# Eight one-bank PSUM tiles instead of four two-bank ones, a third score buffer and an even spread of q·k products in a fused attention and MLP kernel

## The chip, the cores and the metric

One core of a Trainium2 chip runs the whole program. The metric is the device time of one execution in microseconds (us). The engines are TensorE (PE, with its weight loads as PEld), VectorE (DVE), ScalarE (ACT), GpSimd (POOL) and SyncE (SP), which here only issues transfers. TensorE's clock has two levels, 1.2 and 2.4 GHz; the profile gives the granted share (1.00 is 2.4 GHz).

## The reference

Batch 4, 12 heads, 448 tokens, head size 64; then a feed-forward layer of 1792 tokens, 768 to 2048 to 768. All in fp32.

```
scores = scale * q @ k^T                                  # per batch and head
scores = einsum('bhij,hg->bgij', scores, w_pre)           # heads mixed
attn   = softmax(scores, axis=-1)                         # + 1e-9 in the denominator
attn   = einsum('bhij,hg->bgij', attn, w_post)            # heads mixed again
x      = (attn @ v) laid out as (1792, 768)
h      = relu(x @ w_in);  out = (s * h * h + b) @ w_out
```

## The kernel before

**Attention** is a software pipeline. The tokens of a batch are cut into 4 chunks of up to 120 queries (16 chunks), a chunk into blocks of 10 queries (180 blocks), and a step takes two blocks (90 steps). For a chunk, `qk` multiplies q and k of two heads into the PSUM tile `sc`, and `s_copy` (L479, ACT) scales them into the SBUF tile `S`, which holds a chunk's 12 heads in two buffers. `relayout` (L523) moves a block from `S` by DMA into one of six tiles `blk`, so that heads and queries lie on partitions; even blocks go through SP's queue, odd ones through POOL's, three steps ahead of use. A step s then does, in the order in which the code is written:

- `premix` (L533, PE): `blk` times the Kronecker matrix of w_pre into the PSUM tile `pm` (two blocks of columns, b = 0 and 1)
- `av` (L496, PE): the product with v for an earlier chunk, into the PSUM tile `xp`, which takes the slot of the *next* step's `pm`; `tr_q`, `tr_k` (L440, L420, PE): transposes of q and k into slot D
- `maxima` (L542, DVE, one reduction for b = 0 and one for b = 1), `exponential` b = 0 (L548, ACT), `weights` of the step before (L559 reciprocal on DVE, L561 on POOL)
- `x_copies` (L506 on ACT, then L507 on DVE adds the other half), copies of the transposes (L452 ACT, L455 DVE), `exponential` b = 1
- `postmix` (L575, PE) of step s - 2 into `po` (slot C), `evacuate` (L586, DVE, twice), `qk` into slot D, whose copy comes at the start of the next step; `totals` (L554, POOL), DMA issues, and at most two operations of a weight conversion (DVE).

Each engine takes its instructions in this order. The table `plan` says which q·k product, transpose, load and product with v belongs to which step.

**PSUM** has eight banks. The kernel has four slots A to D, each *one tile* `[P, 2, 512]` of two banks. Waits are made per tile: who writes one half of a tile waits for the reader of the other half if that comes earlier in the program.

**The MLP** follows, in two rounds r of 8 blocks f of 128 hidden units. fp32 weights are split into two fp32r parts by a chain of eight DVE operations a unit (`conversion`, L155 to L179), 64 units in 16 buffers. `gemm1_part` (L261) makes `ph` (18 matmuls), `relu2` reads it (L269 ACT and three more ACT operations), `gemm2` (L315) makes `po` for a block of 128 tokens (24 matmuls), read by ACT (L322, r = 0) or DVE (L326, r = 1). `bank` hands out the two halves of a slot in turn.

Of the kernel before, what the change touches and what calls it, by code (L numbers as in the profile page):

```python
# [2 lines left out]

# [18 lines left out]
def talking_heads_attention__then__act_relu2_kernel(  # L22
# [54 lines left out]
    NU_EARLY, NU_TAIL = 7, 6  # L77
# [11 lines left out]
    sp = att.enter_context(tc.tile_pool(name="sp", bufs=2))  # L89
# [150 lines left out]
    turn = {"slot": 0, "half": 1, "ops": 0}  # L240

    def slot(tag, name):
        return ps.tile([P, 2, 512], F32, tag=tag, name=name, bufs=1)
# [44 lines left out]
    def head_piece():  # L288
# [3 lines left out]
        if kc == 0:  # L292
            if f % 2 == 0:
                head_t["two"] = slot("DA"[f // 2], f"ph_head{f}")
            head_t[f] = head_t["two"][:, f % 2]
# [8 lines left out]
    def gemm2(r, oh, its):  # L304

        if len(its) > 1:
            turn["half"] = 1
# [106 lines left out]
    def tr_k(b, p, tr):  # L414
        nat = nat_t.pop((b, p))
        for c in range(NC):
            for r in range(2):
                if c < KC[r]:
                    for e in range(2):
                        nc.tensor.matmul(  # L420
                            tr[64 * e:64 * e + 64, r, 64 * c:64 * c + 64],
# [5 lines left out]
        return [(t[:, HK * r:HK * r + 64 * KC[r]], tr[:, r, :64 * KC[r]]) for r in range(2)]  # L427

    def tr_q(ci, p0, p1, tr):
# [7 lines left out]
        for p in range(p0, p1):  # L437
            for r in range(2):
                for e in range(2):
                    nc.tensor.matmul(  # L440
                        tr[64 * e:64 * e + 64, r, (p - p0) * m[r]:(p - p0 + 1) * m[r]],
# [5 lines left out]
             tr[:, r, :(p1 - p0) * m[r]].rearrange("q (a n) -> q a n", n=m[r]))  # L447
# [11 lines left out]
    def qk(ci, p, sc):  # L459
# [5 lines left out]
        for c0, c1 in ((0, 64), (64, n)):  # L465
            for e in range(2):
                nc.tensor.matmul(  # L467
                    sc[c0:c1, e, :S], qt[64 * e:64 * e + 64, p, c0:c1], kt[64 * e:64 * e + 64, :],
                    start=True, stop=True,
                )  # L470

    def s_copy(ci, p, sc, apart=False):
        n = chunks[ci][2]
        s = s_t[ci]
        if apart:
            nc.scalar.activation(s[:n, 2 * p, :], sc[:n, 0, :S], AF.Copy, scale=SCALE)
            nc.vector.tensor_scalar_mul(s[:n, 2 * p + 1, :], sc[:n, 1, :S], SCALE)
        else:
            nc.scalar.activation(s[:n, 2 * p:2 * p + 2, :], sc[:n, :, :S], AF.Copy, scale=SCALE)  # L479

    def av(ci, p, xp):
# [4 lines left out]
        for i, c in enumerate((0, 3, 1, 2)):  # L486
            for r in range(2):
                for e in range(2):
                    k0, h = 64 * r, 2 * p + e
                    o = xp[64 * e:64 * e + 64, r, :2 * m]  # L490
# [9 lines left out]
    def x_copies(ci, p, xp):  # L500
# [4 lines left out]
        x = [xp[:, r, :BI * nb].rearrange("q (b t i) -> q b t i", b=2, i=UI) for r in range(2)]  # L505
# [383 lines left out]
```

## Time and profile before

| | |
|---|---|
| time, three runs | 1013.74 us (median), 1009.86, 1019.23 |
| profiled execution | 1011.67 us, of which span 1009.9 us |
| PE busy | 835.9 us (83% of the span) |
| DVE, ACT, POOL busy | 537.6 (53%), 436.7 (43%), 243.9 (24%) |
| chain that ended last | PE 60%, DVE 13%, ACT 11%, issue 7%, DMA 7% |
| first `pm`, start of the last step's `pm` | 22.99 us, 446.63 us |
| first matmul of the MLP without the attention beside it | 476.57 us |

Shares of busy time are averages over the two halves. Idle time that a row names is that of one engine just before an instruction, with what ended it. A step of the attention is read as the distance from one `pm` to the next.

### The profile page before, as it was taken

What the parts mean: (1) busy time and instruction counts of PE and PEld (TensorE: products, weight loads), DVE (VectorE), ACT (ScalarE), POOL (GpSimd) and SP (SyncE); (2) the same over time, 40 slices, a digit from 0 to 9 for tenths busy, and PEclk for the clock granted to TensorE, in tenths of its full rate; (3) what the DMA queues carried; (4) which work ended last, traced back from release to release, by engine and by line L of the source; (5) the groups of instructions that cost most, each with busy time, mean ns of one, the idle gap of its engine ahead of it and who ended that gap; (6) DMA issues with size and microseconds to landing.
All of it is one profiled execution on the core that took longest, in us unless ns stands there. A gap on an engine that the chain in (4) does not pass through costs nothing.

```text
span 1009.9 us, 31606 instructions
## 1 busy us (share of the span) xinstructions
PE 835.9 (83%) x13544; PEld 682.5 (68%) x13544; DVE 537.6 (53%) x1186; ACT 436.7 (43%) x935; POOL 243.9 (24%) x446
## 2 busy tenths in 40 slices
PE   7777787677876787795998899799999898996998
PEld 3344555444554554474887789788888787896887
DVE  4465666456656666676930579354039209936111
ACT  4554564455555564544566660110156667300000
POOL 2333343234433433431223230000013223200000
PEclk9899999999999999998999999899999999998999
DMA  5675456644666456741330223425104201434221
GB/s 126 175 183 153 116 130 168 164 143 120 160 167 172 121 146 152 210 121 50 102 104 14 87 79 86 133 91 176 41 15 148 87 1 50 151 107 137 82 93 41
DMA packets 108830, 116.12 MB, mean 115 GB/s; under 512 B 48526, under 2 KB 101130, under 8 KB 108690
## 3 DMA queue, kind: packets, MB, share of 16 engines
q1 hardware_dynamic: 92460, 83.86, 30.4%
q0 software_dynamic: 7120, 18.67, 7.1%
q10 hardware_dynamic: 9110, 11.59, 3.2%
q8 instruction: 106, 1.74, 0.7%
q14 instruction: 34, 0.28, 0.1%
HBM read 58.99 MB, written 16.52 MB: 75 GB/s over the span
## 4 chain that ended last, share of the span: by engine, by line
PE 60%; DVE 13%; ACT 11%; issue 7%; DMA 7%; SPq 2%; ACTq 0%; DVEq 0%
PE ph L261 22%; PE po L315 22%; DVE st L542 5%; PE pm L533 5%; PE sc L467 4%; DMA blk<-S 3%; PE xp L496 3%; ACT e L548 3%; ACT xs L506 2%; ACT h L269 2%; DVE xs L507 2%; DVE A L586 1%; DMA part<-ob 1%; ACT S L479 1%; PE po L575 1%
## 5 line engine op out<-in xcount | busy, mean ns | idle before, releaser
L315 PE MATMUL po<-w,g 128*128 128x384 f32 x1344 | 242.8, 341 | 25.4 <-DVE acc L326 13.3
L315 PEld LDWEIGHTS po<-w,g 128*128 128x128 f32 x1344 | 236.2, 191 | 31.9 <-DVE acc L326 16.5
L261 PE MATMUL ph<-x,w 128*128 128x448 f32 x810 | 170.6, 367 | 20.8 <-ACT h L269 20.8
L261 PEld LDWEIGHTS ph<-x,w 128*128 128x128 f32 x810 | 151.5, 189 | 38.7 <-ACT h L269 28.6
L548 ACT ACTIVATE e<-pm,st 128x448 f32<-128x448 f32 x180 | 113.9, 633 | 115.9 <-DVE st L559 108.6
L279 POOL TENSOR_TENSOR g<-h,g 128x448 fp32r<-128x448 f32 x64 | 79.6, 1243 | 343.7 <-ACT g L278 321.9
L467 PE MATMUL sc<-Tk,Tq 64*64 64x448 f32 (+2 forms) x768 | 96.8, 565 | 54.7 <-ACT Tk L452 22.0
L542 DVE TENSOR_REDUCE st<-pm 128x1 f32<-128x448 f32 x180 | 103.8, 618 | 42.8 <-PE pm L533 32.1
L533 PE MATMUL pm<-blk,wpre 64*64 64x448 f32 x720 | 92.3, 565 | 27.2 <-DVE xs L507 22.1
L496 PEld LDWEIGHTS xp<-A,v 64*64 64x64 f32 x3072 | 77.9, 136 | 45.5 <-issue 33.7
L561 POOL TENSOR_SCALAR W<-kron,st 128x60 f32<-128x60 f32 x180 | 76.4, 431 | 122.7 <-DVE st L559 121.7
L575 PE MATMUL po<-W,e 60*64 60x60 f32 x5040 | 95.4, 219 | 8.8 <-issue 6.9
L586 DVE COPY A<-po 128x420 f32<-128x420 f32 x180 | 98.3, 589 | 7.8 <-PE po L575 7.6
L575 PEld LDWEIGHTS po<-W,e 60*64 60x64 f32 x5040 | 89.5, 136 | 18.4 <-issue 17.1
L479 ACT ACTIVATE S<-sc 110x896 f32<-110x896 f32 (+1 forms) x86 | 79.5, 924 | 44.0 <-DMA blk<-S 22.0
L507 DVE TENSOR_TENSOR xs<-xp,xs 128x110 f32<-128x110 f32 (+1 forms) x96 | 34.0, 354 | 116.3 <-ACT xs L506 116.3
L496 PE MATMUL xp<-A,v 64*64 64x110 f32 (+3 forms) x3072 | 85.8, 250 | 3.8 <-ACT e L548 2.6
L261 PE MATMUL ph<-xg,w 128*128 128x448 f32 x288 | 64.8, 382 | 17.7 <-DVE xg L237 10.0
L237 DVE TENSOR_TENSOR x<-xraw,x 128x448 fp32r<-128x448 f32 x36 | 22.1, 638 | 101.4 <-ACT x L228 101.4
L533 PEld LDWEIGHTS pm<-blk,wpre 64*64 64x64 f32 x720 | 24.1, 135 | 76.6 <-DVE xs L507 49.6
L261 PEld LDWEIGHTS ph<-xg,w 128*128 128x128 f32 x288 | 56.3, 198 | 25.0 <-ACT h L269 10.3
L269 ACT ACTIVATE h<-ph 128x448 f32<-128x448 f32 x61 | 33.1, 542 | 85.3 <-PE ph L261 85.2
(69 smaller groups left out, 787.1 us busy)
## 6 DMA issues: line engine op xcount, KB each, us to landing
blk<-S SPq DMA_DIRECT2D x89, 210.0 KB
blk<-S POOLq DMA_DIRECT2D x83, 210.0 KB, 4.7
raw<-in_moe_w_in_dram SPq DMA_DIRECT2D x32, 384.0 KB
raw<-in_moe_w_out_dram SPq DMA_DIRECT2D x32, 384.0 KB
xraw<-xd SPq DMA_DIRECT2D x48, 224.0 KB
part<-ob ACTq DMA_DIRECT2D x28, 192.0 KB
acc<-part SPq DMA_DIRECT2D x28, 192.0 KB
out_dram<-acc ACTq DMA_DIRECT2D x28, 192.0 KB
```

Source lines behind the costliest of these rows:

```text
L261: nc.tensor.matmul(ph[:, :S], w[:, i, c0:c0 + P], x[:, y, :], start=(kc == 0 and m == 0), stop=(kc == NKC - 1 and m == 2),)
L279: nc.gpsimd.tensor_tensor(out=g[:, 1, c0:c0 + S], in0=h, in1=g[:, 0, c0:c0 + S].bitcast(F32), op=ALU.subtract)
L315: nc.tensor.matmul(po[:, :NO], g[:, x, c0:c0 + P], w[:, y, :], start=(f == 0 and m == 0), stop=(f == NF - 1 and m == 2),)
L467: nc.tensor.matmul(sc[c0:c1, e, :S], qt[64 * e:64 * e + 64, p, c0:c1], kt[64 * e:64 * e + 64, :], start=True, stop=True,)
L479: nc.scalar.activation(s[:n, 2 * p:2 * p + 2, :], sc[:n, :, :S], AF.Copy, scale=SCALE)
L496: nc.tensor.matmul(o, vt[k0:k0 + 64, e, c, :], x, start=(i == 0), stop=(i == NC - 1),)
L533: nc.tensor.matmul(pm[64 * c:64 * c + 64, b, :S], wpre[k, :], blk[k, :], start=True, stop=True)
L542: nc.vector.tensor_reduce(out=st[:, b:b + 1], in_=pm_t[s][:, b, :S], axis=AX.X, op=ALU.max, negate=True)
L548: nc.scalar.activation(e[:, b, :], pm_t[s][:, b, :S], AF.Exp, bias=st[:, b:b + 1], accum_out=st[:, 2 + b:3 + b])
L561: nc.gpsimd.tensor_scalar(w[:, b, :], kron2, st[:, 6 + b:7 + b], None, op0=ALU.mult)
L575: nc.tensor.matmul(po[64 * c:64 * c + 64, r, m * U:m * U + U], e[64 * r:64 * r + U, b, j0:j0 + 64], w[64 * r:64 * r + U, b, :], start=True ...
L586: nc.vector.tensor_copy(a_t[ci].rearrange("q m h j -> q (m h) j")[:, :, UI * r:UI * r + UI], po_t[t // 2][:, t % 2, :n].rearrange("q (m i) ...
```

## The change

- A slot is now a list of two tiles of one bank each; `bank` hands out eight single banks in turn. `maxima` becomes `maximum(s, b)`, and the second stands behind the reciprocal on DVE.
- `x_copies` returns its two parts with keys 0 and 2, copies of transposes get key 1, `s_copy` key 3; what a step has of them is done in the order of the keys. `s_copy` is now two ACT operations of 448 columns in place of one of 896.
- `S` has three buffers (21.5 KB a partition more); 2 instead of 6 weight units (`NU_TAIL`) lie in the space of q and k, the others in the space of the attention.
- The q·k products of chunks 2 to 15 are spread evenly from step 2 to step 80, with their transposes and loads. Before, each chunk had a step without a product and mostly one with two (`more`).

By the two plans, after the change 39 of the 90 steps have one product and nothing else beside their work, 13 have one k transpose, 11 a q transpose; 10 have two things at once (two products, two `av`, two transposes). The first 8 steps have no `av`, steps 81 to 83 no product, and the last 6 carry the first matmuls of the MLP.

```
-    sp = att.enter_context(tc.tile_pool(name="sp", bufs=2))
+    sp = att.enter_context(tc.tile_pool(name="sp", bufs=3))
...
-    NU_EARLY, NU_TAIL = 7, 6
+    NU_EARLY, NU_TAIL = 7, 2
...
+    def one(tag, name):
+        return ps.tile([P, 512], F32, tag=tag, name=name, bufs=1)
     def slot(tag, name):
-        return ps.tile([P, 2, 512], F32, tag=tag, name=name, bufs=1)
+        return [one(f"{tag}{i}", f"{name}_{i}") for i in range(2)]
...
     def bank(name):
-        turn["half"] ^= 1
-        if turn["half"] == 0:
-            turn["two"] = next_slot(name)
-        return turn["two"][:, turn["half"]]
+        turn["bank"] += 1
+        return one(banks[(turn["bank"] - 1) % len(banks)], name)
...
-            nc.scalar.activation(s[:n, 2 * p:2 * p + 2, :], sc[:n, :, :S], AF.Copy, scale=SCALE)
+            for e in range(2):
+                nc.scalar.activation(s[:n, 2 * p + e, :], sc[e][:n, :S], AF.Copy, scale=SCALE)
...
-        nc.scalar.activation(o, x[0], AF.Copy)
-        nc.vector.tensor_tensor(out=o, in0=x[1], in1=o, op=ALU.add)
-        stores.append((xd[b][p, :, n0:n0 + n], xs[:, :n]))
+        def add():
+            nc.vector.tensor_tensor(out=o, in0=x[1], in1=o, op=ALU.add)
+            stores.append((xd[b][p, :, n0:n0 + n], xs[:, :n]))
+        return (0, lambda: nc.scalar.activation(o, x[0], AF.Copy)), (2, add)
...
-        where = [lo + x for x in ([0, 1, 2, 2, 3, 4] if hi - lo < 5 else range(6))]
...
+            step = 2 + ((ci - 2) * NP + p) * (LAST_QK - 2) // ((NCH - 2) * NP - 1)
+            if (step, "qk") in plan:
+                plan[step, "more"] = plan.pop((step, "qk"))
+            at(step, "qk", ci, p)
...
         if s < NS:
-            maxima(s)
+            open_softmax(s)
+            maximum(s, 0)
             exponential(s, 0)
         if 0 <= s - 1 < NS:
             weights(s - 1)
-        for tag in list(users):
-            for f in users.pop(tag):
-                f()
+        if s < NS:
+            maximum(s, 1)
+        for _, f in sorted(sum(users.values(), []), key=lambda x: x[0]):
+            f()
         if s < NS:
             exponential(s, 1)
```

The order of DVE around step 80, a step with one product and one `av`: first the kernel before, then the changed one (`st` maxima and sums, `pm` scores in PSUM, `xp` and `xs` the product with v, `A` the mixed attention; `waits` names whose semaphore is waited for).

```order
L542 TENSOR_REDUCE st_80_7472<-pm_80_7450 128x1 [waits DVE_49,PE_49]
L542 TENSOR_REDUCE st_80_7472<-pm_80_7450 128x1
L559 RECIPROCAL st_79_7396<-st_79_7396 128x2 [waits Pool_49]
L507 TENSOR_TENSOR xs_12_5_7481<-xp_12_5_7455,xs_12_5_7481 128x2x11x5 [waits DMAHW0_49,Activation_49]
L586 COPY A_13_7121<-po_78_7485 128x84x5 [waits PE_49]
L586 COPY A_14_7515<-po_78_7485 128x84x5
```

```order
L546 TENSOR_REDUCE st_80_7933<-pm_80_0_7908 128x1 [waits DVE_49,PE_49]
L563 RECIPROCAL st_79_7852<-st_79_7852 128x2 [waits Pool_49]
L546 TENSOR_REDUCE st_80_7933<-pm_80_1_7909 128x1 [waits PE_49]
L508 TENSOR_TENSOR xs_12_5_7932<-xp_12_5_1_7915,xs_12_5_7932 128x2x11x5 [waits DMAHW0_49,PE_49,Activation_49]
L590 COPY A_13_7557<-po_78_0_7945 128x84x5 [waits PE_49]
L590 COPY A_14_7976<-po_78_1_7946 128x84x5 [waits PE_49]
```

The reciprocal has moved between the two maxima, and each of these now has a PSUM tile and a wait of its own.

The order of ACT in a step with a k transpose (`Tk` is the transposed k, `tr` its PSUM tile), before and changed:

```order
L548 ACTIVATE e_62_5943,st_62_5942<-pm_62_5904,st_62_5942 128x448 [waits PE_49,DVE_49,Activation_49,Pool_49]
L506 ACTIVATE xs_9_4_5951<-xp_9_4_5909 128x2x11x5 [waits DMAHW0_49,PE_49]
L452 ACTIVATE Tk_3_5_5941<-tr_62_5926 128x192 [waits DVE_49]
L548 ACTIVATE e_62_5943,st_62_5942<-pm_62_5904,st_62_5942 128x448
L479 ACTIVATE S_12_5687<-sc_12_4_5988 110x896 [waits PE_49]
```

```order
L552 ACTIVATE e_61_6226,st_61_6225<-pm_61_0_6183,st_61_6225 128x448 [waits DVE_49,Activation_49,Pool_49]
L511 ACTIVATE xs_9_3_6207<-xp_9_3_0_6189 128x2x11x5 [waits DMAHW6_49,PE_49]
L451 ACTIVATE Tk_3_5_6224<-tr_61_1_6209 128x192 [waits PE_49]
L552 ACTIVATE e_61_6226,st_61_6225<-pm_61_1_6184,st_61_6225 128x448 [waits DVE_49]
L479 ACTIVATE S_12_5959<-sc_12_3_0_6271 110x448 [waits PE_49]
L479 ACTIVATE S_12_5959<-sc_12_3_1_6272 110x448 [waits PE_49]
```

The copy of `Tk` waited for DVE (the copy of the other half of the same tile) and now waits for PE alone; the second exponential has a wait of its own; the copy of the scores has become two.

The order of PE in the MLP, around the third product of batch 2 in round 0 (`ph` is the product; before, one name stands for the two halves of a tile):

```order
L261 MATMUL ph_0_2_1_9079<-x_0_2_4_8995,w_3_3886 128x448 x3
L261 MATMUL ph_0_2_1_9079<-x_0_2_5_9001,w_3_3886 128x448 x3
L261 MATMUL ph_0_2_1_9079<-x_0_2_0_8971,w_4_4752 128x448 [waits Activation_49]
L261 MATMUL ph_0_2_1_9079<-x_0_2_0_8971,w_4_4752 128x448 x2
L261 MATMUL ph_0_2_1_9079<-x_0_2_1_8977,w_4_4752 128x448 x3
```

```order
L264 MATMUL ph_0_2_1_9588<-x_0_2_4_9503,w_3_4129 128x448 x3
L264 MATMUL ph_0_2_1_9588<-x_0_2_5_9509,w_3_4129 128x448 x3
L264 MATMUL ph_0_2_2_9614<-x_0_2_0_9479,w_4_5056 128x448 x3
L264 MATMUL ph_0_2_2_9614<-x_0_2_1_9485,w_4_5056 128x448 x3
```

The wait for ACT at the start of the second of two products is gone.

## Rows read from the trace of the kernel before

**Rows 1.** Windows: us, busy PE, PEld, DVE, ACT, POOL, clock, DMA share, GB/s.
```profile
260.00:328.00 68.00, 50.94 (x1636) 34.90 (x1640) 41.21 (x99) 37.59 (x92) 23.48 (x53) 0.97 0.68 173
...
sum 423.00, PE 323.17 PEld 214.35 DVE 259.17 ACT 228.38 POOL 155.81; mean PE 35.91 PEld 23.82 DVE 28.80 ACT 25.38 POOL 17.31
```

**Rows 2.** Timeline of a plain step (start, us, engine, line, operation; [idle before <- releaser]).
```profile
410.05 0.98 PE L533 MATMUL pm<-blk,wpre 64*64 64x448 f32 x8 [0.53 <-DVE xs L507]
...
411.12 1.16 DVE L542 TENSOR_REDUCE st<-pm 128x1 f32<-128x448 f32 x2
...
412.35 0.94 PE L467 MATMUL sc<-Tk,Tq 64*64 64x448 f32 x8
412.40 0.63 ACT L548 ACTIVATE e<-pm,st 128x448 f32<-128x448 f32 x1 [1.46 <-DVE st L559]
...
413.02 0.35 ACT L506 ACTIVATE xs<-xp 128x110 f32<-128x110 f32 x1
...
413.40 0.35 DVE L507 TENSOR_TENSOR xs<-xp,xs 128x110 f32<-128x110 f32 x1 [1.05 <-ACT xs L506]
413.66 1.09 DVE L586 COPY A<-po 128x420 f32<-128x420 f32 x2
...
413.77 0.92 ACT L479 ACTIVATE S<-sc 118x896 f32<-118x896 f32 x1
...
413.81 0.98 PE L533 MATMUL pm<-blk,wpre 64*64 64x448 f32 x8 [0.53 <-DVE xs L507]
```

**Rows 3.** Timeline of a step with a k transpose.
```profile
328.12 0.92 PE L533 MATMUL pm<-blk,wpre 64*64 64x448 f32 x8
...
332.14 0.33 ACT L452 ACTIVATE Tk<-tr 128x192 f32<-128x192 f32 x1 [0.74 <-DVE Tk L455]
...
332.52 0.97 PE L467 MATMUL sc<-Tk,Tq 64*64 64x448 f32 x8 [1.53 <-ACT Tk L452]
...
333.32 0.92 PE L533 MATMUL pm<-blk,wpre 64*64 64x448 f32 x8
```

**Rows 4.** Who waited for whom from 446 us on: total, times, longest.
```profile
PE ph L261 <- ACT h L269: 28.5, 28, 3.5
...
PE po L315 <- DVE acc L326: 13.3, 10, 7.4
...
PE po L315 <- ACT ob L322: 12.2, 10, 6.9
```

**Rows 5.** Windows of the MLP (columns as in Rows 1).
```profile
573.00:640.00 67.00, 64.53 (x348) 61.49 (x346) 58.81 (x129) 24.55 (x43) 10.01 (x8) 1.00 0.35 100
646.50:651.30 4.80, 4.75 (x15) 4.75 (x16) 0.00 (x0) 0.00 (x1) 0.00 (x0) 0.50 0.11 41
```

**Rows 6.** Timeline of another step: a weight conversion, a q transpose.
```profile
337.89 0.56 DVE L169 SCALAR_TENSOR_TENSOR w<-mk,u 128x384 fp32r<-128x384 f32 x1
...
338.52 0.87 PE L440 MATMUL tr<-ident,nq 64*64 64x64 f32 x48
```

**Rows 7.** Timeline of SP's queue in a step that loads v.
```profile
381.14 0.54 SPq L514 DMA_DIRECT2D xd<-xs  x1
381.79 0.85 SPq L523 DMA_DIRECT2D blk<-S  x1
382.69 2.92 SPq L379 DMA_DIRECT2D v<-in_v_dram  x2
385.65 0.62 SPq L391 DMA_DIRECT2D v<-in_v_dram  x1
```

**Rows 8.** DMA issues: operation, KB each, us to landing.
```profile
blk<-S POOLq DMA_DIRECT2D x83, 210.0 KB, 4.7
```

**Rows 9.** Who waited for whom from 23 to 446 us.
```profile
ACT S L479 <- DMA blk<-S: 22.0, 6, 5.4
```

**Rows 10.** Timeline: starts of two neighbouring steps with loads, PE.
```profile
173.83 0.98 PE L533 MATMUL pm<-blk,wpre 64*64 64x448 f32 x8 [0.44 <-DVE xs L507]
...
181.85 1.71 PE L533 MATMUL pm<-blk,wpre 64*64 64x448 f32 x8
```

More of the change, by code (lines that the diff above doesn't have):

```diff
@@ L2 @@
 from contextlib import ExitStack
+from functools import partial
 import concourse.bass as bass
@@ L239, in talking_heads_attention__then__act_relu2_kernel @@
     slots = ["A", "B", "C", "D"]
-    turn = {"slot": 0, "half": 1, "ops": 0}
+    banks = [x + y for x in slots for y in "01"]
+    turn = {"slot": 0, "bank": 0, "ops": 0}
+    def one(tag, name):
+        return ps.tile([P, 512], F32, tag=tag, name=name, bufs=1)
     def slot(tag, name):
-        return ps.tile([P, 2, 512], F32, tag=tag, name=name, bufs=1)
+        return [one(f"{tag}{i}", f"{name}_{i}") for i in range(2)]
     def next_slot(name):
@@ L426, in tr_k @@
         k_t[b, p] = t
-        return [(t[:, HK * r:HK * r + 64 * KC[r]], tr[:, r, :64 * KC[r]]) for r in range(2)]
+        return [(t[:, HK * r:HK * r + 64 * KC[r]], tr[r][:, :64 * KC[r]]) for r in range(2)]
     def tr_q(ci, p0, p1, tr):
@@ L533, in premix, with open_softmax @@
                 nc.tensor.matmul(
-                    pm[64 * c:64 * c + 64, b, :S], wpre[k, :], blk[k, :], start=True, stop=True
+                    pm[b][64 * c:64 * c + 64, :S], wpre[k, :], blk[k, :], start=True, stop=True
                 )
-    def maxima(s):
+    def open_softmax(s):
         st = smp.tile([P, 8], F32, tag="st", name=f"st_{s}")
@@ L540, in maxima, with maximum @@
         e_t[s] = (e, st)
-        for b in range(2):
-            nc.vector.tensor_reduce(
-                out=st[:, b:b + 1], in_=pm_t[s][:, b, :S], axis=AX.X, op=ALU.max, negate=True
-            )
+    def maximum(s, b):
+        nc.vector.tensor_reduce(
+            out=e_t[s][1][:, b:b + 1], in_=pm_t[s][b][:, :S], axis=AX.X, op=ALU.max, negate=True
+        )
     def exponential(s, b):
@@ L604, in talking_heads_attention__then__act_relu2_kernel @@
     at(1, "qk", 1, 5)
[L605 removed]
+    LAST_QK = first[NCH - 1] // 2 - LDS - 1
     for ci in range(2, NCH):
         b = chunks[ci][0]
[L608 to L609 removed]
         news = chunks[ci - 1][0] != b
[L611 removed]
         for p in range(NP):
[L613 to L622 removed]
+            step = 2 + ((ci - 2) * NP + p) * (LAST_QK - 2) // ((NCH - 2) * NP - 1)
+            assert step <= first[ci] // 2 - LDS - 1
+            if (step, "qk") in plan:
+                plan[step, "more"] = plan.pop((step, "qk"))
+            at(step, "qk", ci, p)
+            if p == 0:
+                at(step - 3 if news else step - 1, "tr", tr_q, ci, 0, NP)
+                if ci > 2:
+                    at(step - 7 if news else step - 5, "load", load_q, ci)
+            if news:
+                at(step - 2, "tr", tr_k, b, p)
+                at(step - 5, "load", load_k, b, p)
     for ci in range(NCH):
@@ L780, in talking_heads_attention__then__act_relu2_kernel @@
     assert not plan, plan
-    turn["slot"], turn["half"] = 1, 1
+    turn["bank"] = 2
     att.close()
```

54 lines of the change are left out of this document (18 added, 36 removed).

## The prediction

> **What bounds the kernel now.** I read the page first, for the shares; then windows, to see that the two halves differ; then the timeline of single steps, and the waits of each half. Between 23 and 446 us the attention runs 89 of its 90 steps. PE is busy for 323 of these 423 us, DVE for 259, ACT for 228 [rows 1]: no engine is full, so the step is a chain from engine to engine. In a plain step [rows 2] the reader can walk round it. The mixed scores `pm` start at 410.05. DVE begins its two maxima at 411.12 and takes 1.16 for both. The first exponential starts at 412.40, ACT's half of `xs` at 413.02, DVE's at 413.40, and the next `pm`, which takes the banks that `xs` has just left, at 413.81. The loop is 3.76 us, and PE sat idle for 0.53 of it. A step with a k transpose takes 5.20 (328.12 to 333.32): ACT's copy of the transpose waits 0.74 for DVE's copy of the other half, and the q·k product, in the same two banks, 1.53 for ACT's [rows 3]. In the MLP PE is nearly full, and what it waits for is always the reader of a PSUM tile: 28 times ACT's first operation on `ph` (28.5 us), 20 times the readers of `po` (13.3 and 12.2) [rows 4]. That is one pause for every second product; the first half of a tile is still being read when PE wants the second half.
>
> **The change in the MLP.** With one tile a bank, these 48 pauses have no cause: the order rows show the second product without a wait, and a bank comes round again after eight products. Removed: 28.5 + 13.3 + 12.2 = 54.0 us, all on PE, which sets the end there. What is late next? DVE's weight conversions are no faster; in the densest stretch, 573 to 640 us, DVE is busy for 58.8 of 67 us and PE for 64.5 without waiting for it [rows 5], so I charge nothing; if that cover went, a conversion late by some us each in 57 units would eat the gain. The longest pauses (up to 7.4 us) are followed by a stretch at 1.2 GHz: 4.8 us of nothing but matmuls at a granted clock of 0.50 [rows 5], in which 2.4 us of work is lost. Of the pauses, four are over 3 us (two in each round); at 0 to 2.4 each I take 7 us for the four. Sum for the MLP: 61 us, bounds 45 (a few of the pauses stay, no clock) and 64. The gap between the halves, where PE waits for the split of x behind two conversions on DVE, stays: those stand in the same order.
>
> The Trainium skill has a rule that speaks against this part (TensorE: Matmul & The Clock Gate, A second HAM failure mode: psum-queue depth-cycling): a kernel that cycled through PSUM banks left PE idle in small pieces, and its clock swung between the two levels. In this trace the clock is 1.00 from 573 to 640 us [rows 5], a stretch with such pauses between products, and it fell only after the long ones; the trace does not bear the rule out. By the rows the MLP gains 61 us; by that rule, with eight banks to cycle through, what the pauses give would be lost in clock again, and the sum would be without the 61 (rival D).
>
> **The change in the attention.** (1) *Maxima apart.* The first exponential no longer waits for the second maximum. Half of 1.16 leaves the loop: 3.76 - 0.58 = 3.18. The second maximum (0.58) and the short reciprocal now lie beside the exponential and ACT's `xs` (412.40 to 413.40, 1.0 us), so DVE is free when its half of `xs` is due. PE needs, from `pm` to the product q·k, 2.30 (410.05 to 412.35) and from there to the next `pm` 0.80 (332.52 to 333.32) [rows 2, 3]: 3.10, just under the loop. DVE's copies of `A` (413.66 for 1.09) end when `pm` does, so whatever DVE does after them delays the next maximum: 49 operations of weight conversion of about 0.56 [rows 6] in some 70 steps, 0.39 a step. Before, the waits elsewhere hid part; I take 0.27 a step, bounds 0 and 0.39: 3.45 for a plain step. (2) *Transposes.* The copies of the two banks no longer wait for each other, nor behind the addition of `xs`. What is left is PE: a k transpose is 28 matmuls, and 48 of the q transpose took 0.87 [rows 6], so 0.51; 3.10 + 0.51 = 3.61, with the copy's own latency 3.75 instead of 5.20. A step with a q transpose, now with a product beside it: 3.10 + 0.87 = 3.97, I take 4.05. (3) *Spread.* The number of products is the same; steps without one are filled and most double steps go. (4) *Copies of the scores* cost ACT more: two of 448 columns against one of 896 at 0.92; the exponential of that width takes 0.63 [rows 2], so at most 2 x 0.63 - 0.92 = 0.34 more, 29 us for 86. ACT was busy 228 of 423 us [rows 1] and would be at some 257 of 360, and the copy lies ahead of an exponential that waits for DVE anyway (1.46 idle, rows 2). Charged at nothing; if that idle time were gone, the bound is 29 us.
>
> Adding up 89 steps: 39 plain at 3.45 (134.6), 3 without a product at 3.25 (9.8), 13 with a k transpose at 3.75 (48.8), 11 with a q transpose at 4.05 (44.6), 10 with two things at once at 4.55, an estimate from a plain step and one more product or `av` of about a microsecond (45.5), the first 8, which have no `av` but wait for blocks, at 3.6, an estimate near the plain step (28.8), 5 of the last 6, which carry six more matmuls each, at 4.1 (20.5): 332 against 423, so 91 us by the engines alone.
>
> **What gives part of it back.** The transfers do not shrink. In a step that loads v, SP's queue is busy for 0.54 + 0.85 + 2.92 + 0.62 = 4.93 us [rows 7], more than the step would now take. There are 18 such steps besides the first six: at most 18 x (4.93 - 3.6) = 24 us, at least nothing, since blocks are ordered three steps ahead and part of SP's time is itself waiting for room. The stretch from 260 to 328 us moves 0.68 x 68 = 46 us of full DMA work [rows 1] and would be squeezed into about 49 us. I take 14 us for SP and DMA together. A block is ordered at the end of a step for the third step after it, so about two steps remain: 2 x 4.75 = 9.5 us before (423/89), 2 x 3.7 = 7.4 after. Through POOL it lands 4.7 us after its issue [rows 8], a median; I take 12 us for blocks that come late, and for what a late one costs in clock; bounds 0 and 30. The third buffer of S takes away six waits of ACT for the DMAs that empty it, 22.0 us [rows 9]; since the steps above are priced without such waits, that is in the 91 already. Attention: 91 - 14 - 12 = 65 us, bounds 37 (24 and 30 given back) and 91.
>
> **Sum.** From the profiled execution, 1011.67 - 61 - 65 = 886 us. The profiled execution lies 2 us under the median of the three runs, which spread over 9 us, so I say 887.
>
> **Rivals.** *A, as above:* both halves gain. 860 to 912 us. *B, the queue takes the attention's gain:* SP's queue and late blocks set the step wherever something is loaded. For it: 4.93 us of SP in a step; against: the same queue stands idle in the stretches without loads. Attention 25 us, the lower bound above and some PE clock, so 1011.67 - 61 - 25 = 926. *C, the engines alone set the step:* backlog is absorbed by the three steps of lead. 1011.67 - 61 - 91 = 860; for it, that DMA reached its present share with steps that waited for other things. *D, the banks bring nothing in the MLP,* because PE's pauses come back as something else (weights, clock): 1011.67 - 65 = 947. Against it: the wait is gone in the order rows, DVE keeps up, and the clock was full [rows 5]. *E, slower than before:* with shorter steps every block comes late wherever something is loaded. The step at 173.83 took 8.0 us [rows 10], PE's next products 1.71 instead of 0.98. Against 3.6 that is 4.4 lost a step. By the engines alone the change brings 61 + 91 = 152, so it decides from 152/4.4 = 35 such steps on; of the steps after the first six, 42 load q, k or v, and all of them would give 1011.67 - 152 + 185 = 1045. Against it: such a step was rare, and part of it was the wait for `S` [rows 9], which goes. *F, it does not do what it says:* only if the tiles of one bank were still waited for in pairs; the order rows exclude it.
>
> **How the numbers follow.** A 0.62, B 0.16, C 0.11, D 0.05, E 0.03, the rest, F (no change), 0.03. The range takes in A (860 to 912), C and half of B: 858 to 928, which leaves out less than 2 in 10. For faster by over 1% (about what a measurement of this kernel tells from no change) A to D count: 0.94; within 1% 0.03; slower 0.03.
>
> **What would show it.** Right: PE's waits for L269's, L322's and L326's successors on `ph` and `po` gone, no stretch at 0.50 after 500 us; plain steps at 3.2 to 3.5; k-transpose steps under 4; `xs` following the first exponential with DVE not late. Wrong: SP's queue never idle and `pm` waiting for the DMA of `blk` (B, E); `pm` waiting for the copies of scores on ACT (the split copy on the path); a new wait of PE for weights in the MLP (D).

## The result, and the profile after

The changed kernel takes 901.50 us (median of 4 runs, 900.07 to 903.12) against 1013.94 (1009.86 to 1019.23): ratio 0.889, 95% interval 0.885 to 0.893. The profiled execution is 900.07 us, its span 898.4.

The sum came out 14 us below the measurement, but its two halves were both off, in opposite directions. From the first `pm` to that of the last step the attention now takes 387.8 us (21.99 to 409.83), before 423.6: 35.8 gained where 65 were forecast. From there to the end it takes 488.6 us, before 563.3: 74.7 gained where 61 were forecast. The start is 1.0 earlier.

The page after: PE fills nearly every slice of the second half, and the clock falls in the first.

```profile
span 898.4 us, 31636 instructions
...
PE 826.0 (92%) x13544; PEld 710.1 (79%) x13544; DVE 544.9 (61%) x1186; ACT 439.4 (49%) x1021; POOL 238.9 (27%) x446
...
PE   7779988789979898899599999999999999999998
...
PEclk9978999989989999999799999999999999999999
```

PE's waits from 411 us to the end (total, times, longest), which answer to [rows 4], and two stretches of the MLP, which answer to [rows 5]:

```profile
PE ph L264 <- DVE xg L238: 9.8, 1, 9.8
PE po L579 <- ACT xs L511: 0.5, 1, 0.5
```
```profile
573.00:640.00 67.00, 67.00 (x389) 67.00 (x388) 37.60 (x92) 10.82 (x22) 0.00 (x0) 1.00 0.49 161
640.00:655.00 15.00, 15.00 (x88) 15.00 (x87) 0.00 (x0) 1.96 (x4) 0.00 (x0) 1.00 0.11 40
```

All 48 pauses before `ph` and `po` are gone; the gap between the halves stays, as forecast. PE is busy without a hole, at the full clock.

The timeline of a plain step after, which answers to [rows 2]:

```profile
135.64 1.02 PE L536 MATMUL pm<-blk,wpre 64*64 64x448 f32 x8
...
136.69 0.62 DVE L546 TENSOR_REDUCE st<-pm 128x1 f32<-128x448 f32 x1 [0.41 <-PE pm L536]
...
137.17 0.98 PE L579 MATMUL po<-W,e 60*64 60x60 f32 x53
...
137.31 0.60 DVE L546 TENSOR_REDUCE st<-pm 128x1 f32<-128x448 f32 x1
137.43 0.63 ACT L552 ACTIVATE e<-pm,st 128x448 f32<-128x448 f32 x1 [0.52 <-DVE st L563]
...
137.94 0.54 PE L466 MATMUL sc<-Tk,Tq 64*64 64x448 f32 x1
...
138.06 0.36 ACT L511 ACTIVATE xs<-xp 128x120 f32<-128x120 f32 x1
...
138.46 0.37 DVE L508 TENSOR_TENSOR xs<-xp,xs 128x120 f32<-128x120 f32 x1 [0.55 <-ACT xs L511]
...
138.70 1.16 PE L536 MATMUL pm<-blk,wpre 64*64 64x448 f32 x8
```

The exponential starts 1.79 us behind `pm` instead of 2.35, and the step takes 3.06 with no idle time of PE ahead of `pm`. The timeline of a step with a k transpose, the answer to [rows 3], where the product no longer waits for the copies:

```profile
286.04 1.24 PE L536 MATMUL pm<-blk,wpre 64*64 64x448 f32 x8
...
288.49 0.42 DVE L454 COPY Tk<-tr 128x256 f32<-128x256 f32 x1
...
288.87 0.37 ACT L451 ACTIVATE Tk<-tr 128x192 f32<-128x192 f32 x1
288.96 0.59 PE L466 MATMUL sc<-Tk,Tq 64*64 64x448 f32 x1
...
289.76 0.54 PE L536 MATMUL pm<-blk,wpre 64*64 64x448 f32 x1
```

Such steps (3.06 and 3.72) lie at or under the prediction's prices (3.45 and 3.75). Many others are slower. PE's waits between 22 and 410 us show why:

```profile
PE pm L536 <- DMA blk<-S: 25.7, 15, 3.6
PE po L579 <- issue: 10.8, 16, 1.9
PE tr L439 <- issue: 4.3, 3, 2.1
PE xp L496 <- issue: 3.4, 4, 1.1
...
PE sc L466 <- issue: 1.3, 1, 1.3
```

Late blocks cost 25.7 us (4.9 before), and 19.8 us are "issue", pauses that nothing in the profile releases. PE ran at half clock (granted clock 0.50) for 34 us of the attention (17 before), which loses about 17. The trace tells which waits this goes with: six of the seven stretches, 30.6 of the 34 us, begin during or at most 1.2 us after the six longest waits for a block (1.99 to 3.58 us). Only one, of 3.4 us, follows a pause of the "issue" kind (1.07 us, at 81.9). The eighteen such pauses from 121 to 163 us and from 292 to 359 us (up to 2.07 us) were followed by no fall of the clock.

Mean step by kind, as forecast, in the changed kernel, and in the run without loads (below):

| steps | forecast | after | without loads |
|---|---|---|---|
| 39 plain | 3.45 | 3.94 (median 3.65) | 3.45 |
| 13 with a k transpose | 3.75 | 4.52 | 4.23 |
| 11 with a q transpose | 4.05 | 5.20 | 4.58 |
| 10 with two things | 4.55 | 5.25 | 5.22 |
| first 8 | 3.6 | 4.32 | 4.51 |
| 3 without a product, 5 of the last 6 | 3.25, 4.1 | 3.13, 4.35 | 3.51, 5.00 |
| sum | 332 | 387.8 | 363.6 |

### The profile page after: what moved, and what is told of

The parts are those of the page before. It is cut to its first block, busy times and chain, and to the rows that moved or that the text cites. A ratio compares the mean times of both kernels' runs of the same rounds, so it can differ in the third digit from the quotient of the medians.

```text
span 898.4 us, 31636 instructions
## 1 busy us (share of the span) xinstructions
PE 826.0 (92%) x13544; PEld 710.1 (79%) x13544; DVE 544.9 (61%) x1186; ACT 439.4 (49%) x1021; POOL 238.9 (27%) x446
## 3 DMA queue, kind: packets, MB, share of 16 engines
q8 instruction: 107, 1.75, 0.8%
## 4 chain that ended last, share of the span: by engine, by line
PE 84%; DMA 7%; issue 3%; DVE 2%; SPq 2%; ACT 1%; ACTq 0%; POOL 0%; DVEq 0%
PE po L314 26%; PE ph L264 25%; PE xp L496 8%; PE pm L536 7%; PE po L579 7%; PE sc L466 7%; DMA blk<-S 6%; PE ph_head L264 1%; PE tr L439 1%; PE tr L419 1%; SPq L409 1%; DMA nk<-in_k_dram 1%; SPq L378 0%; ACT xs L511 0%; DVE st L546 0%
## 5 line engine op out<-in xcount | busy, mean ns | idle before, releaser
L314 PE MATMUL po<-w,g 128*128 128x384 f32 x1344 | 233.3, 336 | 0.0
L264 PEld LDWEIGHTS ph<-x,w 128*128 128x128 f32 x810 | 151.9, 188 | 10.2
L536 PE MATMUL pm<-blk,wpre 64*64 64x448 f32 (+1 forms) x720 | 105.0, 566 | 28.3 <-DMA blk<-S 25.7
L496 PEld LDWEIGHTS xp<-A,v 64*64 64x64 f32 x3072 | 95.1, 138 | 34.7 <-issue 24.3
L579 PE MATMUL po<-W,e 60*64 60x60 f32 x5040 | 109.2, 225 | 12.5 <-issue 10.8
L579 PEld LDWEIGHTS po<-W,e 60*64 60x64 f32 x5040 | 101.1, 140 | 20.0 <-issue 18.5
L466 PE MATMUL sc<-Tk,Tq 64*64 64x448 f32 (+2 forms) x768 | 106.2, 558 | 4.6 <-DVE Tq L454 1.6
L496 PE MATMUL xp<-A,v 64*64 64x110 f32 (+3 forms) x3072 | 102.8, 254 | 3.8 <-issue 3.4
L479 ACT ACTIVATE S<-sc 110x448 f32<-110x448 f32 (+1 forms) x172 | 84.3, 543 | 43.2 <-PE sc L466 40.6
L536 PEld LDWEIGHTS pm<-blk,wpre 64*64 64x64 f32 (+1 forms) x720 | 35.4, 136 | 71.5 <-DMA blk<-S 22.9
L526 POOL DMA_DIRECT2D blk<-S x87 | 56.5, 649 | 32.1 <-PE sc L466 11.9
L238 DVE TENSOR_TENSOR x<-xraw,x 128x448 fp32r<-128x448 f32 x36 | 21.5, 622 | 68.2 <-ACT x L229 68.2
```

What stands on the lines that cost most here:

```text
L264: nc.tensor.matmul(ph[:, :S], w[:, i, c0:c0 + P], x[:, y, :], start=(kc == 0 and m == 0), stop=(kc == NKC - 1 and m == 2),)
L314: nc.tensor.matmul(po[:, :NO], g[:, x, c0:c0 + P], w[:, y, :], start=(f == 0 and m == 0), stop=(f == NF - 1 and m == 2),)
L466: nc.tensor.matmul(sc[e][c0:c1, :S], qt[64 * e:64 * e + 64, p, c0:c1], kt[64 * e:64 * e + 64, :], start=True, stop=True,)
L479: nc.scalar.activation(s[:n, 2 * p + e, :], sc[e][:n, :S], AF.Copy, scale=SCALE)
L496: nc.tensor.matmul(o, vt[k0:k0 + 64, e, c, :], x, start=(i == 0), stop=(i == NC - 1),)
L536: nc.tensor.matmul(pm[b][64 * c:64 * c + 64, :S], wpre[k, :], blk[k, :], start=True, stop=True)
```

## Pauses without a releaser: PE's own instructions

The trace holds PE's code as transfers: the queue "instruction" (q8) brings 107 packets, 1.75 MB, 16 KB each; the program's 27,088 matmuls and weight loads with 251 waits make 256 instructions a packet (in e8, with fewer matmuls, 21,489 make 84 packets, again 256 each). I numbered PE's matmuls, weight loads and waits in the order of their starts and looked where it stood still (of the changed kernel; worked out from the trace's records):

```
PE idle          us    next   number mod 256   last packet landed   from there
125.28-126.68   1.41   L579        194              125.22             1.46
148.32-150.38   2.07   L439        194              148.96             1.42
226.56-228.44   1.89   L439        193              226.92             1.52
301.25-302.56   1.30   L579        194              301.11             1.45
345.20-347.07   1.86   L579        194              345.74             1.33
```

In the middle of a row of matmuls PE stops, always at the same number of a block of 256 (give or take one), and goes on 1.2 to 1.7 us after a packet has landed. The first of these in the timeline of PE:

```profile
125.05 0.23 PE L579 MATMUL po<-W,e 60*64 60x60 f32 x2
126.68 0.97 PE L579 MATMUL po<-W,e 60*64 60x60 f32 x50 [1.41 <-issue]
```

There are 29 such pauses, 20.9 us, in the changed kernel's attention, and 12, 10.1 us, in that of before. From 60 to 405 us a packet mostly starts to arrive after PE has begun the block before it: 1.3 us later in the median, 4.8 at most; four come ahead of it, by up to 0.8 us. In the changed kernel 50 of 74 blocks of 256 (from 60 to 405 us) began within 1.7 us of their packet's landing, 16 of 66 before. Where PE was so held, a block took 4.13 us in the median (2.9 at least, so that this is no fixed rate), 16 ns an instruction. A plain step has 208 instructions (3.36 us at that rate), one with a k transpose 264 (4.26), one with a q transpose 304 (4.90).

The Trainium skill (Runtime: NRT & Kernel Launch, Instruction fetch mechanics) says that the sequencer fetches its code in blocks of 16 KiB, 256 instructions, ahead of use, and calls the cost mostly hidden. The size agrees with the trace (1.75 MB in 107 packets). That the cost is hidden does not hold for this attention: 20.9 us in 29 pauses.

## The experiments

Ratios are to the kernel before, with 95% intervals; the attention is read from the profiled executions. Where kernels share the code of the attention, it still differs by some 6 us from one profile to the next, so less than that is not told apart there. For each run: the instructions of PE in the attention (matmuls, weight loads and waits), its pauses at the border of a block of 256, all its idle time, and the length of the attention.

```
                      PE instr   pauses    us    idle   attention
before                 20,712      12     10.1  100.0    423.6
after                  20,722      29     20.9   53.2    387.8
e1  all blocks, POOL   20,728      42     37.2   59.1    396.1
e2  no loads           20,647      26     20.1   36.3    363.6
e8  wider matmuls      15,192       1      0.3    7.1    421.9
e10 128 partitions     18,657      15     11.9   41.1    391.1
e11 lead of four       20,737      34     28.8   56.6    392.0
e14 early loads        20,709      39     30.2   52.9    382.5
```

What is left of the attention without PE's idle time and without what half clock loses is PE's own time for its matmuls: 315 us before, 318 after, 321 in e2, but 341 in e10 and 411 in e8.

**Late blocks: the queue, or the transfers?** All blocks through POOL:

```
-    queue = nc.gpsimd if t % 2 and t > 2 * LDS else nc.sync
+    queue = nc.gpsimd if t > 2 * LDS else nc.sync
```

> The changed kernel, but all blocks from the seventh on are moved through POOL's queue, the even ones too, which went through SP's. In the changed kernel PE waits 25.9 us in 15 places for a block between its 22nd and its 410th microsecond. Theory Q (the blocks are late because they stand behind loads of q, k and v in SP's queue): these waits fall under 8 us, a part of the 34 us at half clock goes with them, 866 to 882 us. Rival T (the transfers themselves are the limit, 16 DMA engines at about 0.6 in those stretches): the blocks land no earlier, 895 to 906. Rival P (88 more issues of 0.65 us on POOL, in order with the weights W and the totals that the path needs): W comes late, PE waits for POOL, 905 to 930.

907.93 us (ratio 0.894, 0.890 to 0.898). PE's waits:

```profile
PE po L579 <- issue: 20.3, 21, 2.8
PE xp L496 <- issue: 9.8, 8, 2.5
PE pm L536 <- DMA blk<-S: 5.7, 9, 1.7
```

Four fifths of the waits for blocks are gone, so what made them late was SP's queue and not the transfers; yet nothing is gained, and theory Q's 866 to 882 us are missed. The time lies in rival P's range, but PE waits for the weights W from POOL for only 0.6 us: the pauses at packets have taken the place (37.2 instead of 20.9 us), with one late load of q (5.7). None of the three theories had that.

**What the loads cost in all.**

```
     def load_v(b, p, queue=nc.sync):
...
+        if b > 0:
+            v_t[b, p] = t
+            return
...
     def load_k(b, p, queue=nc.sync):
+        if b > 0:
+            nat_t[b, p] = keep_nk[0]
+            return
...
     def load_q(ci):
+        if ci > 3:
+            nat_t[ci] = nat_t[3]
+            return
```

> The changed kernel without the loads of k and v of batches 1 to 3 and of q from chunk 4 on (it uses what is already there, so this part of the computation is left out). Theories Q and T alike: the waits of PE for blocks (25.9 us) go, with what they cost in clock, some 12 us. Theory I (PE stands still 28 times, 20 us in all, because its own instructions come late, in packets of 16 KB, one for every 256 instructions): if what makes the packets late is the traffic of loads, these pauses go as well, 840 to 850 us; if it is PE's rate alone, they stay at 15 to 25 us, 858 to 868.

875.12 us (0.862, 0.858 to 0.865), 26.4 below the changed kernel; the prediction had charged 14 + 12 = 26 for queue, late blocks and their clock. The waits for blocks fall from 25.7 to 9.9 us, and what half clock loses from 17.0 to 6.8. The pauses at packets stay (20.1 us), so leaving out the traffic of the loads does not take them away. And 363.6 us of attention without the later loads of q, k and v are 32 more than the 332 that the engines were to need.

```profile
PE po L591 <- issue: 12.0, 11, 2.3
PE pm L548 <- DMA blk<-S: 9.9, 6, 2.9
PE xp L508 <- issue: 5.5, 7, 2.2
```

**Fewer instructions, wider matmuls.**

```
-        for c0, c1 in ((0, 64), (64, n)):
...
+                sc[e][:n, :S], qt[64 * e:64 * e + 64, p, :n], kt[64 * e:64 * e + 64, :],
...
+                        po[r][:, m * U:m * U + U],
+                        e[64 * r:64 * r + U, b, P * j:P * j + P], w[64 * r:64 * r + U, b, :],
```

> The changed kernel with fewer and wider matmuls for the same products: q.k in 2 of up to 118 columns of weights instead of 4 of 64 or less, the second mixing in 16 instead of 28 (the columns of k stand in another order for it), q's transposes in 12 instead of 24. PE's instructions in a plain step go from 208 to 152. Theory I (PE's code comes in packets of 256 instructions that are usable about 4 us after the packet before was begun): the 20 us of pauses without a releaser fall under 4 us and plain steps lose what the packets held them to, 866 to 885 us. Rival W (wider matmuls leave fewer of them side by side in the array, so PE's own time grows by up to 0.4 us a step): 905 to 935. Rival N (the pauses come from something else): they stay, 893 to 903.

941.53 us (0.929, 0.923 to 0.936). One pause of 0.3 us is left of 20.9, and 2.7 us of waits for blocks: with 152 instructions in 4.3 us neither limit binds. But rival W holds, by more than it said (935 at most). So the run does not show what the pauses are worth: they went together with a longer step of PE. A plain step of PE:

```profile
355.69 0.98 PE L538 MATMUL pm<-blk,wpre 64*64 64x448 f32 x8
356.50 0.86 PE L498 MATMUL xp<-A,v 64*64 64x110 f32 x32
357.29 1.55 PE L577 MATMUL po<-W,e 60*128 60x60 f32 x24
358.77 0.34 PE L585 MATMUL po<-W,e 60*64 60x60 f32 x8
359.04 1.01 PE L468 MATMUL sc<-Tk,Tq 64*110 64x448 f32 x4
359.98 0.98 PE L538 MATMUL pm<-blk,wpre 64*64 64x448 f32 x8
```

The 24 wide matmuls of the second mixing take 1.48 us (62 ns each); in the plain step above, 53 narrow ones take 0.77 from start to start (137.17 to 137.94), about 15 ns each. One wide matmul in place of two narrow ones took twice their time.

**Summing over 128 partitions** in the product with v, 10 matmuls instead of 16:

```
+                    vt[:, e, c, :], a[:, c:c + NC:NC - 1, h, :m],
```

> The changed kernel with the product with v in 10 matmuls a step instead of 16: three of four key chunks are summed over 128 partitions at once instead of 64 and 64 in two banks (the addition of xs then covers half the columns). PE's instructions in a plain step go from 208 to 184, the work in the array is the same. Theory I (in 50 of 74 packets of 256 instructions PE began a packet as soon as it was there, 4.1 us a packet in the middle): a tenth fewer packets, 866 to 885 us, and fewer pauses without a releaser. Rival W (as with the wider matmuls: fewer lie side by side in the array): this part of PE's step grows from 0.86 to as much as 1.5 us, 915 to 945. Rival N (no limit of this kind): 896 to 905.

906.09 us (0.898, 0.893 to 0.902): a tenth fewer instructions, pauses down from 20.9 to 11.9 us, but PE's own steady step is up from 3.06 to 3.35, and the sum is the same within a few us. The trace shows where that comes from: the product with v, from its start to the bulk of the second mixing, takes 1.04 us (111.85 to 112.89) where it took 0.77 in the changed kernel (136.40 to 137.17). That is the growth that rival W said, at a smaller size; that fewer matmuls lie side by side is not shown. None of the three ranges was met, though N's ends 1 us below the measurement, and what the pauses are worth is again not told apart from the longer step.

**One more step of lead for the blocks.**

```
-    LDS, NBLK, LAG = 3, 6, 2
+    LDS, NBLK, LAG = 4, 8, 2
...
```

Room for it is made elsewhere: W has two buffers instead of three, the small tiles (`smp`) three instead of four, and one converted weight unit less lies ready.

> The changed kernel with blocks ordered four steps ahead instead of three, in eight buffers instead of six (the products of q and k one step earlier; for the room one converted weight unit less lies ready, and W has two buffers instead of three). Blocks keep their queues, so POOL has no more to do than before, other than in the run that moved all blocks to POOL. Theory Q alone (late blocks are what the attention loses): the 25.9 us of waits and a part of the half-clock stretches go, 866 to 884 us. Theory I (PE's own instruction packets are the next limit behind them): the waits for blocks go under 10 us, but pauses at packets grow from 22 to 30 us or more, 888 to 902 us. Rival: SP's queue never catches up, so a step of lead only moves the lateness: over 898 with the waits for blocks still above 18 us.

902.89 us (0.891, 0.888 to 0.893), a microsecond above the range of theory I. The blocks are in time (2.4 us), the pauses at packets grow to 28.8 (30 or more were expected), and the loads that stand behind the blocks in SP's queue are late now:

```profile
PE tr L439 <- DMA nq<-in_q_dram: 9.3, 2, 5.2
...
PE tr L419 <- DMA nk<-in_k_dram: 7.5, 4, 4.0
...
PE pm L536 <- DMA blk<-S: 2.4, 2, 2.0
```

**The same, with the loads pulled apart.**

```
+                    at((step - 7 if news else step - 5) - 3 * (ci > 4), "load", load_q, ci)
+                at(step - 5 - 10 * (ci > 4 and p < 4), "load", load_k, b, p)
```

> The run with four steps of lead, and in it the loads of q (from chunk 5 on) three steps earlier and of the first four pairs of heads of k (batches 2 and 3) ten steps earlier, so that they no longer fall into the steps that load v. In the run with four steps of lead PE waited 16.8 us for loads of q and k, 2.4 us for blocks, and 28 us at the borders of its instruction packets. Theory B (a burst in SP's queue makes loads or blocks late, whichever stands behind): both waits fall under 6 us together, and 880 to 892 us. Rival I (PE's instruction packets take what is freed, as they did in the run with four steps of lead and in the one with all blocks on POOL): the waits go, the packet pauses grow past 33 us, 894 to 904 us. Rival T (the transfers themselves fill the DMA engines): the waits stay above 12 us, 898 to 906 us.

892.94 us (889.73 to 896.45; ratio 0.882, 0.879 to 0.885, against 0.889, 0.885 to 0.893 for the changed kernel): about 8 us faster than the change, at the edge of what the intervals tell apart. Waits for k are down to 0.7 us and for blocks to 1.5; two for q stay (10.0, at 41.9 and 61.5 us, for chunks whose loads were not moved); packets take 30.2. The attention is 9.5 us shorter than with the lead alone: 6.8 fewer of waits for k, and half-clock stretches of 20.5 us instead of 37.5, against 1.4 more at packets. None of the three ranges was met: B wanted both waits under 6 us, I pauses over 33. B holds for the loads that were moved, and the largest part of what stays is what I names.

**Which part of the change gives what.** Only the tiles of one bank, with the split copies of scores and the order of copies by key (old table, two `S`, both maxima first):

```
             maximum(s, 0)
+            maximum(s, 1)
             exponential(s, 0)
...
-    NU_EARLY, NU_TAIL = 7, 2
+    NU_EARLY, NU_TAIL = 7, 6
-    sp = att.enter_context(tc.tile_pool(name="sp", bufs=3))
+    sp = att.enter_context(tc.tile_pool(name="sp", bufs=2))
...
+        where = [lo + x for x in ([0, 1, 2, 2, 3, 4] if hi - lo < 5 else range(6))]
```

> Of the change only the tiles of one bank (with the split copy of scores and the order of a step's copies by key): the old table of products, two buffers of scores and both maxima ahead of the exponential. The MLP gains what it gained in the changed kernel, 75 us. Theory: the one-bank tiles carry nearly all of the attention's 36 us too (copies of transposes and of xs that no longer wait for one another), because undoing the spread or the order of the maxima alone moved the time by 3 us at most: 900 to 915 us. Rival: spread, third buffer and maxima stand in for each other and bring most of the attention's gain only together: 922 to 940 us.

912.05 us (0.901, 0.899 to 0.903), inside the theory's 900 to 915: some 101 of the 112 us. The attention is at 397.5, 26 of the 36 us. ACT's copies of scores wait for their buffer again (35.2 us), and PE for the copies (11.3).

The spread alone undone (the last line of that diff without the others):

> The changed kernel with the table of q.k products, transposes and loads as it was before (the spread alone undone). By the prediction's prices for steps, 9 steps with two products at 4.55 and fewer plain ones give 340 instead of 332 us of steps: 905 to 914 us. Rival: the spread is worth more, because a chunk's products come in a burst that the third buffer of scores can't use, and ACT waits for the buffer again: 915 to 930, with waits of the score copies for the blocks' DMAs. Rival: the spread is worth nothing (bound by PE's instruction packets or blocks either way): 898 to 904.

904.29 us (0.891, 0.887 to 0.894), 3 above: the price by kinds of steps gave 8, and the result is nearest to the rival by which the spread is worth nothing. The third buffer alone undone (the two pairs of lines in the middle of that diff):

> The changed kernel with two buffers of scores S instead of three (and six units of weights in the room of q and k again). With products spread evenly, a copy of scores then waits for the blocks of two chunks before to leave the buffer. Theory S (the third buffer is what took away before's 22.0 us of ACT waiting for the blocks' transfers, and the spread needs it more): such waits return on ACT and pm or the products wait behind them, 910 to 930 us. Rival: the waits return on ACT, but lie beside PE's own limits (late blocks, instruction packets): 898 to 906 us.

945.51 us (943.05 to 956.11; 0.935, 0.930 to 0.941), 44 above the changed kernel and 33 above the banks alone, more than either range said: with products spread evenly and two buffers, the copies of a new chunk wait for the blocks of the chunk before last. Of its profiled execution, the longest of the four (PE's wait is counted up to 410 us, of an attention that ends at 467):

```profile
ACT S L479 <- DMA blk<-S: 49.5, 8, 11.3
```
```profile
PE sc L466 <- ACT S L479: 40.9, 11, 7.8
```

Its attention is 57 us longer than the changed kernel's (444.4 against 387.8); 24 of these are clock, 81.6 us at 0.50 instead of 34. So the third buffer is worth 8 us or less with the old table (904 against 912, with the order of the maxima in it) and 44 with the spread. Both maxima first again (its first lines):

> The changed kernel with both maxima ahead of the first exponential again, in the order of before; everything else as changed. Theory L (the loop from engine to engine that the prediction walked round sets a plain step): its 0.58 us comes back in the steps that now take 3.0 to 3.4 us, about 45 of them, and the addition of xs is late again: 915 to 928 us. Rival I (PE's instruction packets and late blocks set most steps, the loop has slack): 901 to 908.

899.37 us (895.59 to 904.13; 0.890, 0.884 to 0.895): no change. But the edit took away less than its text says. Also with both maxima first, the exponential starts behind the first of them:

```profile
138.23 1.16 DVE L546 TENSOR_REDUCE st<-pm 128x1 f32<-128x448 f32 x2 [0.41 <-PE pm L536]
```
```profile
138.97 0.63 ACT L552 ACTIVATE e<-pm,st 128x448 f32<-128x448 f32 x1 [0.52 <-DVE st L546]
```

0.74 us after the first maximum's start, while the second runs until 139.39. The wait for both did not go with the order in the code. With the banks alone (e13), where both maxima stand first too, the exponential also starts 0.74 us after the first maximum's start (132.20 to 132.94); so it went with the one-bank tiles. This run, then, does not test theory L; it shows only that the order is worth nothing.

**What a pause costs in the MLP.** One bank for all products there (but where eight are open):

```
+    def few(name):
+        turn["few"] = turn.get("few", 0) + 1
+        return one(banks[2 + turn["few"] % 1], name)
...
-                ph = bank(f"ph_{r}_{b}_{f}")
+                ph = one("D1", f"ph_{r}_{b}_{f}") if wait else few(f"ph_{r}_{b}_{f}")
...
-        pos = [bank(f"po2_{r}_{oh}_{it}") for it in its]
+        pos = [(bank if len(its) > 1 else few)(f"po2_{r}_{oh}_{it}") for it in its]
```

> The changed kernel, but in the MLP every product (ph, and po where only one is open) goes to the same bank, so that each waits for the reader of the one before it: about 51 pauses before ph and 38 before po, where the kernel before had 28 and 20 and the changed kernel has none. Theory 'idle as shown': a pause costs what the trace of before shows as idle (0.69 and 0.6 us): 901.5 + 51 x 0.69 + 38 x 0.6 = 960 us. Theory 'idle and restart': a pause costs more, because the matmuls behind it start late too (in before the one after the pause starts 1.06 us behind its predecessor and the next two 0.31 and 0.37, against 0.20 each; for po 0.92 and 0.28 against 0.17): 1.14 and 0.9 us a pause, 901.5 + 58 + 34 = 994 us. Rival 'clock': so many pauses drop the clock to its lower level again and again: over 1030, with many stretches at 0.50.

1010.82 us (0.998, 0.995 to 1.001). PE's waits in the MLP, and a stretch of it:

```profile
PE ph L268 <- ACT h L276: 41.3, 55, 1.1
PE po L318 <- DVE acc L329: 19.6, 19, 6.6
PE po L318 <- ACT ob L325: 16.9, 19, 6.4
```
```profile
500.00:560.00 60.00, 50.95 (x240) 43.68 (x239) 31.46 (x59) 35.95 (x60) 15.86 (x13) 1.00 0.21 59
```

From the last step's `pm` on, this takes 598.0 us against 488.6: 109.4 more for 96 pauses. They are shown as 79.8 us idle, and two stretches at half clock lose 6.8; the other 23 us, 0.24 a pause, stand in no row as idle. The stretch shows it: 240 matmuls at 0.2006 (their mean pitch in the changed kernel, without pauses) are 48.1 us, so 11.9 are lost at twelve pauses, and only 9.05 shown. "Idle and restart" holds, and the total is above its 994, since there were more pauses than I counted and two long ones. The rival "clock" does not: 60 us with a pause after every product ran at 1.00, where the prediction's own evidence, 573 to 640 us of the kernel before, held only three pauses.

That also bears on the rule that the prediction weighed (the Trainium skill, TensorE: Matmul & The Clock Gate, A second HAM failure mode: psum-queue depth-cycling): the clock stayed full with pauses between all products, and with eight banks there were no pauses; neither way does a run here show it.

Two banks in turn (`% 2` in `few`, and `few` for every `ph`):

> The changed kernel, but in the MLP the products rotate over two banks instead of eight (except the eight that are open at once). Theory: only the wait for the reader of the very next product counted, and with two tiles of a bank each that reader (0.54 us) is long done when its bank comes round (3.6 us later): 898 to 905 us, no pause. Rival: the depth of the rotation is what brings the full clock or hides the readers: pauses before ph or po appear, 915 us or more.

918.71 us (0.909, 0.903 to 0.915; two runs): the rival's number, for a reason that I had overlooked. PE idles 11 us at nine places where the reader of a product is issued after the next product (four times before `ph`, 1.1 each) or where eight products were open just before. Elsewhere two banks do.

## Why the prediction was right, and where it was wrong

- **MLP, 61 against 74.7.** The mechanism and the 54.0 us of waits held: all gone, DVE's conversions never late. Mis-sized was the price of a pause: I took the idle time as shown. At the 0.24 us a pause that e6 shows beyond it, the restart adds 11 us for 48; in the kernel before it was not measured by itself. The clock term (7) was 10: the four stretches after 500 us last 20.5 us at half clock. 54 + 11 + 10 = 75; another 1 us of the 74.7 was won between the last `pm` and the first product behind the gap.
- **Maxima.** The exponential comes 0.56 earlier (0.58 forecast), and a plain step free of other trouble takes 3.38 in the mean (25 of the 39, with under 0.3 us of idle PE and the full clock, 3.0 to 3.9). The cause was the tile, not the order that the prediction named (e3, e13).
- **Transposes.** Undisturbed steps with a k transpose take 3.76 in the mean of six (3.75 forecast), the copies no longer wait for one another. Split score copies: two take 0.98 for one of 0.92, and products wait 0.4 us for them in all; charging nothing was right, the bound of 29 us far too wide.
- **332 us for the engines alone: the step that failed.** It added PE's matmuls as if their instructions were always there. PE's own time is 315 to 321 us before, after and without the loads, so 332 left 11 to 17 us for all idle time and low clock. Without the later loads the same steps take 363.6, with 36 us of idle time, 20.1 of it pauses at packets and 9.9 for blocks, and 6.8 lost at half clock. Of the 31.6 us too many, some 19 lie in the steps with transposes or two things, which have the most instructions, and 7 in the first 8, where the blocks are late. The trace of before had it: 12 pauses, 10.1 us, "issue" in its waits. I did not ask what would happen to them when steps get a fifth shorter (4.75 to 3.7 by the forecast). That the pauses come from late code is read from where they stand and from the packets' landings; what they cost is read from the trace too, since the runs with fewer instructions (e8, e10) lengthened PE's own step.
- **26 us for queue, late blocks and clock** were right in size (26.4 without the later loads), by another split: no queue term of 14 beside the late blocks, but 15.8 us of their waits and 10.2 of their clock. Nor was it a price that can be won back one by one: with the blocks in time (e1, e11) packets and then loads took their place.
- **Third buffer.** The waits of [rows 9] are gone. That the spread costs 33 us without it, I had not seen: I priced spread and buffer apart.
- **The order of rivals.** By its marks the run lies between A and B: A's waits on `ph` and `po` gone, B's waits for blocks there. That the sum came out 14 us off is partly luck: 14 more in the MLP and 29 less in the attention half cancel.

The half clock of the changed kernel goes with its late blocks (30.6 of 34 us), not with its pauses at packets; in e11 and e14, five stretches of 3.4 us did follow pauses of 2.3 to 3.1 us there. What stays open: what the pauses at packets would give back with everything else equal, and what decides when a packet is sent.

## What to carry to other kernels

Before pricing steps by busy time, count instructions: where small matmuls make an engine issue one every 15 ns, its own code becomes a stream that can come late, and a wait that is removed elsewhere can turn into a wait for it (e1, e11). Buffers and schedule are priced together, since an even schedule may need the buffer that an uneven one did without. A total that fits proves little: compare the stages, since two errors may cancel in part.

## What the runs showed of the hardware

- PE's code came in packets of 16 KB for 256 instructions; a block was runnable 1.2 to 1.7 us after its packet landed, and blocks that waited for theirs took 4.1 us in the median. Leaving out 13 of 66 MB of transfers changed the pauses little (20.9 to 20.1 us).
- A stationary side of 128 columns over 64 rows took 62 ns where two of 64 columns took some 30 together (second mixing). The Trainium skill (TensorEngine Tiling (Array Packing), Tiling Modes) lists two such tiles that work side by side, against four of 64 by 64; by that 24 wide ones would take as long as 48 narrow ones. The trace does not show this here.
- A wait between two products cost PE 0.24 us beyond its idle time (e6, 96 waits).
- In the changed kernel's attention the granted clock fell to 0.50 during or just after the six longest waits of PE for a block (1.99 to 3.58 us), and once more behind a pause at a packet.
